# Second part in column halves: every leaf and outer product as two matmuls with 64 columns of weights

## The chip, the cores and the metric

The kernel runs on one core of a Trainium2 chip. What counts is the device time of one launch in microseconds (us), the median of several runs.

## The reference

Random-feature attention over 8 batches, 8 heads, 576 tokens and 64 features a head, then a Fourier mix and a feed-forward block on 8 x 576 = 4608 rows of 512 features, all in float32:

```python
q_p, k_p = phi(q_s), phi(k_s)                      # exp features, 128 of them
num = q_p @ (k_p^T v);  den = q_p @ sum(k_p) + 1e-06
x = num / den                                      # heads side by side: (8, 576, 512)
mixed = real(fft(fft(x, axis=1), axis=2))
u = x + mixed
un = (u - mean(u)) / sqrt(var(u) + 1e-06)
out = u + maximum(un @ w_ch1, 0) @ w_ch2           # 512 -> 2048 -> 512
```

Only the last line's two matrix products matter here.

## The kernel before

The program is written out by a planner of its own (`Listing`): steps with an engine and a planned time, in an order that is fixed by strings of picks. It is then issued in exactly that order, engine by engine, so a change inside a step does not move any other instruction. A matmul in float32 goes to the array as two weight loads and two matmuls, so the profile counts each call of `nc.tensor.matmul` twice; only transposes and bf16 matmuls count once.

The first part (to about 418 us) holds the attention, the Fourier mix, and the feed-forward of the first 4 tiles of 128 rows with plain products (L1236, L1259). The second part holds the feed-forward of the other 4096 rows, in 8 blocks of 512 (`j` = 0 to 7), with a fast matrix product of seven partial products in place of eight, on two levels: seven outer products (`i`), and within each seven inner ones (`n`), called leaves. Sums of weights and tokens are made beforehand by VectorE and GpSimd; the leaves add into PSUM banks, which ScalarE and VectorE copy, seed and combine.

- First layer, `first_of`: a leaf's matmuls contract over 128 input features. Blocks 0 and 1 are done alone: a leaf (L1727) is 4 matmuls with 128 columns of weights and 128 moving columns (tokens). Blocks 2 to 7 are done in pairs (`wide`): a leaf then has 256 moving columns and 2 matmuls, and is done twice (`g`) for the two halves of the hidden features. In block 0 six of the seven outer products have no inner level (`single`): L1878, 16 matmuls each with 256 moving columns.
- Second layer, `product_of`: a leaf (L2178) is 4 matmuls that add into the same 128 columns of a bank; its weights are 128 tokens' hidden values, its moving operand 128 columns of a `wl` tile that SyncE's queue loads (L2074) as buffers come free.

The steps between leaves: ScalarE saves a bank to SBUF (L1752, L2149), seeds another (L1759, L2194), VectorE adds a bank and a saved one (L2154, L1653, L1770), and a later leaf adds into the same bank. The last sums of hidden values (L1683) are on VectorE and GpSimd, tokens' sums on VectorE (L1358, L1456).

Ahead of the first leaves, `washed` (L2298) fills three banks by two bf16 matmuls each, on the whole array: four of the six stand before the first leaf, two after the second leaf.

Column halves and quarters of the array are in use in the first part: L735 and L701 work on quarters (64 rows by 64 columns of weights), L782 and L790 on column halves (128 rows by 64 columns, 65 moving), and L944 for the last group of frequencies on column halves with 128 and 129 moving columns. Two matmuls whose outputs lie in different halves of the partitions lie on different halves of the array's columns.

Of the kernel before, what the change touches and what calls it, by code (L numbers as in the profile page):

```python
# [375 lines left out]
def kernel(  # L376
# [10 lines left out]
    nc = tc.nc  # L387

    B, H, S, D = q.shape
# [13 lines left out]
    P = 128  # L403
# [663 lines left out]
    Q = 32  # L1067
# [45 lines left out]
    def normed(j, pool):  # L1113
# [12 lines left out]
        for i in range(TB // 128):  # L1126
            n, was = i + TB // 128 * (j - head(j)), head(head(j) - 1)
            yield Fork(paced(i), LEAF * (98 * was + 49 * len(unit(was)) * n // 8 - 8))

# [160 lines left out]

    tts = {}
    wxs, so = {}, {}
    LEAF = 0.9
    STORED = (1, 2, 5, 6, 3, 7, 4)
    PARTS = (1, 5, 2, 6, 3, 7, 4)
# [10 lines left out]
    def head(j):  # L1306

        return j - (j - WIDE) % 2 if wide(j) else j
# [380 lines left out]
    def first_of(j, i, g):  # L1689
        me = ("first", j, i, g)  # L1690
        cell_of = partial(here_of(j), g=g)
        span = 2 * P if wide(j) else P
# [16 lines left out]
        def leaf(n, ps, start, after=(), take=(), give=(), makes=None):  # L1709
            own = n in (5, 6, 3) and i != 1  # L1710
            w = ("wx", 1) if i == 1 else ("wx", j, i, n) if own else ("so", i, n)
            if wide(j) and (j, i) != (WIDE, 1):
                m = PARTS.index(n) + 7 * g
                own, w = m % 2, ("wx", j, i, m // 2)
            token = (("tokens", j, i),) if i != 1 else (("tt1" if wide(j) else "tt", j),)
            yield Step(
                PE, 0.866 if wide(j) else 0.895, after=token + (w,) + after, take=take, give=(("wl",) if own else ()) + give,
                makes=makes, bias=LEAF * PARTS.index(n),
            )
            b = None  # L1720
            if take:
                b, ps = got()
            elif isinstance(ps, str):
                ps = kept["y"][1]
            left, right = weights_of(j, i, n, g), tokens(j, i, n)
            for f in range(4 * P // span):
                nc.tensor.matmul(  # L1727
                    ps[:, span * f : span * f + span].rearrange("f (b q) -> f b q", q=Q),
                    lhsT=left[:, P * f : P * f + P],
                    rhs=right,  # L1730
                    start=start and f == 0,
                    stop=True,
                    skip_group_check=True,
                )
            return b, ps

        def made(f, t):
# [74 lines left out]
        if i in single(j):  # L1812
            def cells(n, f, c):
                return hid[:, n, f, :, 256 * c : 256 * c + 256]

            def halves_of(ps):
                return ps.rearrange("p (t n) -> p t n", t=2)


            unseeded = (0,) if not j and i == ORDER0[1] else ()  # L1820

            def out(f, c, b, ps):
                row = tuple(e for t in range(2) for e in over(f, t))
                here = (me, "half", f, c)
                if 2 * f + c in unseeded:
                    yield Step(DVE, 0.7, 0.1, after=free + row + with_(f, 0) + with_(f, 1), give=(b,), makes=here, bias=1.75)
                    relu_sum(cells(slot, f, c), halves_of(ps), cells(addend, f, c))
                    return
                yield Step(ACT, 0.6, 0.1, after=free + row, give=(b,) if i != 5 else (), makes=here, bias=1.75 * (2 * f + c + 1))
                nc.scalar.activation(out=cells(slot, f, c), in_=halves_of(ps), func=AF.Relu if final else AF.Copy)  # L1830

            def u4_of(f, c, b, ps):
                read = ((("second", j - 1, READ["u4"]), "read"),) if j else tuple(
                    ("h", j, n, f, t, g) for n in (2, 6) for t in range(2)
                )
                yield Step(
                    DVE, 0.7, 0.1, after=read + tuple(("h", j, 6, f, t, g) for t in range(2)) + ((me, "half", f, c),),
                    give=(b,), makes=("h", j, "u4 half", f, c), bias=1.75 * (2 * f + c + 1),
                )
                nc.vector.tensor_tensor(out=cells(C12, f, c), in0=halves_of(ps), in1=cells(C21, f, c), op=ALU.add)  # L1840

            def whole(f):
                here = tuple((me, "half", f, c) for c in range(2))
                if i != 5:
                    for t in range(2):
                        yield Step(NONE, after=here, makes=made(f, t))
                else:
                    here = tuple(("h", j, "u4 half", f, c) for c in range(2))
                    for t in range(2):
                        yield Step(NONE, after=here, makes=("h", j, "u4", f, t, g))  # L1850

            def seed_of(k):
                f, c = divmod(k, 2)
                after = with_(f, 0) + with_(f, 1) + (((me, "done", k - 2),) if k > 1 else ())
                yield Step(ACT, 0.6, 0.1, take=("clean",), after=after, makes=(me, "seed", k), bias=1.75 * k - 2)
                kept[k] = got()
                nc.scalar.activation(out=halves_of(kept[k][1]), in_=cells(addend, f, c), func=AF.Copy)

            for k in range(4 * merged):
                if k not in unseeded:  # L1860
                    yield Fork(seed_of(k))
            w, right = outer_weights(i), outer_tokens(j, i)
            for f in range(2):
                for c in range(2):
                    k = 2 * f + c
                    fresh = not merged or k in unseeded
                    seeded = () if fresh else ((me, "seed", k),)
                    yield Step(
                        PE, 1.73, after=(("tt", j),) + tuple(("sum", i, d, f) for d in range(2)) + seeded,
                        take=bank if fresh else (), give=("set",) if f and c else (),  # L1870
                        makes=(me, "done", k), bias=1.75 * k,
                    )
                    b, ps = got() if fresh else kept[k]
                    for n in range(2):
                        cell = ps.rearrange("p (t n) -> p t n", t=2)[:, :, 128 * n : 128 * n + 128]
                        for d in range(2):
                            col = GW * f + 256 * c + 128 * n
                            nc.tensor.matmul(  # L1878
                                cell.rearrange("f t (b q) -> f t b q", q=Q),
                                lhsT=w[:, d, col : col + 128],  # L1880
                                rhs=right[:, :, d].rearrange("f (t b) q -> f t b q", t=2),
                                start=fresh and n == 0 and d == 0,
                                stop=d == 1,
                                skip_group_check=True,
                            )
                    yield Fork(out(f, c, b, ps))
                    if i == 5:
                        yield Fork(u4_of(f, c, b, ps))
                yield Fork(whole(f))
            for n in ("leaves", "y"):  # L1890
                yield Step(NONE, after=((me, "done", 3),), makes=(me, n))
            return
# [80 lines left out]
    def w1_inner():  # L1973
# [19 lines left out]
        def replaced(i, a21):  # L1993
# [3 lines left out]
                makes=("so", i, 7),  # L1997
                bias=LEAF * (30 + 7 * m),
            )
# [31 lines left out]
    wls = {}  # L2031
# [80 lines left out]
    def product_of(j, i, cells):  # L2112
# [48 lines left out]
        def leaf(n, ps, left, start, after=(), give=(), take=(), makes=None):  # L2161

            shared = ((("second", j - 1, i), {5: "p5 read", 4: "read"}.get(n, n)),) if j != head(j) else ()
            yield Step(
                PE,
                0.895,
                after=(("wl", head(j), i, n),) + shared + after,
                take=take,
                give=(() if wide(j) and j == head(j) else tag_of(j, i, n)[:1]) + give,
                makes=makes or (me, n), bias=pace * LEAF * PARTS.index(n),  # L2170
            )
            b = None
            if take:
                b, ps = got()
            elif isinstance(ps, str):
                ps = saved["y"][1]
            for f in range(4):
                nc.tensor.matmul(  # L2178
                    ps[:, 0:128],
                    lhsT=left[:, f],  # L2180
                    rhs=wls[head(j), i, n][:, f],
                    start=start and f == 0,
                    stop=(f == 3),
                    skip_group_check=True,
                )
            return b, ps

        def of_sum(n):
# [206 lines left out]
```

## Time and profile before

| what | us |
|---|---|
| median of 3 runs | 1123.8 |
| lowest and highest | 1123.35, 1124.15 |
| span of the profiled execution | 1119.2 |
| TensorE matmuls busy | 1108.4 |
| TensorE weight loads busy | 1000.4 |
| VectorE busy | 888.7 |
| ScalarE busy | 539.5 |
| GpSimd busy | 390.6 |

The span runs from the first to the last instruction of the profiled execution; no other time is listed for that execution, and the median lies 4.6 us above its span. PE stands for TensorE's matmuls, PEld for its weight loads, DVE for VectorE, ACT for ScalarE, POOL for GpSimd, SPq for SyncE's DMA queue. A row of the timeline gives the start, the time from the first start to the last end, and how many instructions are merged; matmuls overlap, so the distance between starts is smaller than the duration of one. A form such as 128*64 128x129 means 128 rows and 64 columns of the array and a moving operand of 128 partitions and 129 columns.

### The profile page before, as it was taken

The page shows a single profiled execution, that of the slowest core. Times are in us where ns is not written, and L with a number is a line of the kernel's source. Part 1 is how long each engine was busy: PE and PEld are TensorE (multiplying, and loading weights), DVE is VectorE, ACT ScalarE, POOL GpSimd, SP SyncE. Part 2 cuts the span into 40 slices and gives each one's busy share as a digit, 9 for nine tenths or more (in the row PEclk, how much of TensorE's full clock was granted, in tenths as well). Part 3 has the DMA queues.
Part 4 walks back from the last instruction along what each step waited for, and adds up shares of the span by engine and source line. Part 5 has one row for each costly group of instructions (what it writes and reads, how often), then busy time and mean ns, then how long its engine had stood idle before and what let it go on. Part 6 is the DMA issues. An engine that isn't in the chain of part 4 may idle for free.

```text
span 1119.2 us, 31666 instructions
## 1 busy us (share of the span) xinstructions
PE 1108.4 (99%) x12467; PEld 1000.4 (89%) x12467; DVE 888.7 (79%) x1685; ACT 539.5 (48%) x1644; POOL 390.6 (35%) x401
## 2 busy tenths in 40 slices
PE   9999999999999999999999999999999999999998
PEld 7888888879868778999999889999889999889998
DVE  6999999987576767687697777888677888568895
ACT  7998898856536455623214452223463223331221
POOL 2443443553563348634413464000365000152000
PEclk9999999999999999999999999999999999999999
DMA  8856766665674669798896778747678656546453
GB/s 243 243 174 188 242 180 191 183 208 176 216 232 156 194 172 343 224 314 262 260 326 224 226 216 248 207 148 238 206 207 261 207 155 216 170 152 220 146 160 105
DMA packets 196549, 236.13 MB, mean 211 GB/s; under 512 B 53808, under 2 KB 120624, under 8 KB 196400
## 3 DMA queue, kind: packets, MB, share of 16 engines
q1 hardware_dynamic: 195904, 233.83, 68.1%
q8 instruction: 99, 1.62, 0.6%
q14 instruction: 50, 0.41, 0.1%
q10 hardware_dynamic: 496, 0.26, 0.1%
HBM read 182.13 MB, written 56.10 MB: 213 GB/s over the span
## 4 chain that ended last, share of the span: by engine, by line
PE 92%; DVE 3%; ACT 2%; DMA 2%; issue 0%; POOL 0%; SPq 0%; DVEq 0%; ACTq 0%
PE banks L2178 31%; PE banks L1727 27%; PE banks L1236 5%; PE banks L701 5%; PE banks L607 5%; PE banks L1259 5%; PE banks L1878 4%; PE banks L735 3%; PE banks L782 2%; PE banks L944 2%; PE banks L894 1%; ACT e L661 1%; DVE nmx L644 1%; PE banks L904 1%; DMA unw<-turned 1%; DMA raw<-in_moe_w_ch_dram 1%
## 5 line engine op out<-in xcount | busy, mean ns | idle before, releaser
L2178 PE MATMUL banks<-wl,sums 128*128 128x128 f32 x1792 | 219.8, 275 | 0.0
L2178 PEld LDWEIGHTS banks<-wl,sums 128*128 128x128 f32 x1792 | 210.6, 192 | 1.0 <-issue 0.3
L661 ACT ACTIVATE e<-banks,nmx 128x128 f32<-128x128 f32 x576 | 165.7, 441 | 23.3 <-DVE nmx L644 22.9
L644 DVE TENSOR_REDUCE nmx<-banks 128x8 f32<-128x1024 f32 (+1 forms) x96 | 89.3, 951 | 16.8 <-PE banks L701 12.4
L2178 PE MATMUL banks<-wl,hid 128*128 128x128 f32 x768 | 99.2, 275 | 0.3 <-DVE part L2154 0.3
L2178 PEld LDWEIGHTS banks<-wl,hid 128*128 128x128 f32 x768 | 92.8, 192 | 1.2 <-DVE part L2154 0.8
L2149 ACT ACTIVATE s<-banks 128x128 f32<-128x128 f32 x112 | 30.9, 277 | 113.6 <-PE banks L2178 103.5
L1727 PE MATMUL banks<-unw,wxw 128*128 128x256 f32 x352 | 85.4, 379 | 0.0
L701 PE MATMUL banks<-om,kqT 64*64 64x128 f32 (+1 forms) x2088 | 79.0, 275 | 1.7 <-ACT kv L751 1.3
L701 PEld LDWEIGHTS banks<-om,kqT 64*64 64x64 f32 (+1 forms) x2088 | 64.5, 138 | 12.7 <-issue 3.2
L2178 PE MATMUL banks<-wl,hx 128*128 128x128 f32 x576 | 74.2, 275 | 0.4 <-DVE part L2154 0.4
L1727 PEld LDWEIGHTS banks<-unw,wxw 128*128 128x128 f32 x352 | 66.6, 190 | 8.9
L1727 PE MATMUL banks<-rx,wxw 128*128 128x256 f32 x288 | 70.8, 379 | 0.0
L2178 PEld LDWEIGHTS banks<-wl,hx 128*128 128x128 f32 x576 | 69.4, 192 | 0.8 <-DVE part L2154 0.6
L1752 ACT ACTIVATE s<-banks 128x512 f32<-128x512 f32 x65 | 38.5, 596 | 65.1 <-PE banks L1727 60.0
L1727 PE MATMUL banks<-ttw,wxw 128*128 128x256 f32 x288 | 69.8, 379 | 0.0
L1236 PE MATMUL banks<-unT,w 128*128 128x128 f32 x512 | 65.4, 279 | 1.7 <-DVE qeT L621 1.7
L550 POOL TENSOR_TENSOR w<-w,raw 128x512 f32<-128x512 f32 x28 | 37.6, 1351 | 77.3 <-DVE raw L544 68.1
L2227 POOL TENSOR_TENSOR more<-more,part 128x512 f32<-128x512 f32 x2 | 2.6, 1315 | 176.6 <-ACT part L2220 176.6
L1236 PEld LDWEIGHTS banks<-unT,w 128*128 128x128 f32 x512 | 60.2, 192 | 4.5 <-issue 2.3
L1727 PEld LDWEIGHTS banks<-rx,wxw 128*128 128x128 f32 x288 | 54.5, 190 | 7.3
L1727 PEld LDWEIGHTS banks<-ttw,wxw 128*128 128x128 f32 x288 | 54.5, 190 | 7.3
(287 smaller groups left out, 2442.3 us busy)
## 6 DMA issues: line engine op xcount, KB each, us to landing
wl<-w2l SPq DMA_DIRECT2D x245, 256.0 KB, 3.9
wxw<-w1x SPq DMA_DIRECT2D x120, 256.0 KB, 3.1
raw<-in_moe_w_ch_dram SPq DMA_DIRECT2D x32, 512.0 KB, 4.8
kq<-in_k_dram SPq DMA_DIRECT2D x32, 288.0 KB, 4.5
kq<-in_q_dram SPq DMA_DIRECT2D x32, 288.0 KB, 4.5
vd<-in_v_dram SPq DMA_DIRECT2D x32, 288.0 KB, 5.4
ur<-us SPq DMA_DIRECT2D x30, 256.0 KB, 5.2
w2l<-sums SPq DMA_DIRECT2D x14, 512.0 KB, 4.9
```

The lines of the kernel that those rows point to most:

```text
L550: eng.tensor_tensor(out=dst, in0=dst, in1=lof, op=ALU.add)
L607: nc.tensor.transpose(ps[:, (j - j0) * 128 : (j - j0 + 1) * 128], src(j), ident[:])
L644: nc.vector.tensor_reduce(nmx[:, :, 0:num], pps[:, :, 0 : MF * num].rearrange("p b (c m) -> p b c m", m=MF), axis=AX.X, op=ALU.max, negate ...
L661: nc.scalar.activation(out=e[:, c + (i if num == 1 else 0), :], in_=pps[:, i, MF * c : MF * c + MF], func=AF.Exp, bias=nmx[:, i, c : c + 1],)
L701: nc.tensor.matmul(pps[cols, c, MF * m : MF * m + MF], lhsT=kqT[rows, j, cols], rhs=om2[rows, :],)
L735: nc.tensor.matmul(kvp[cols, i, 0 : D + 1], lhsT=feature(r)[rows, cols], rhs=vds[n % NV][rows, r, :], start=(r == 0), stop=(r == R - 1),)
L1236: nc.tensor.matmul(hp[:, 0:TP], lhsT=w1[:, dc, 128 * fc : 128 * fc + 128], rhs=unTs[key][:, dc, :], start=(dc == 0), stop=(dc == NDC - 1),)
L1259: nc.tensor.matmul(yp[:, 0:DM], lhsT=hs[fc][:, 128 * i : 128 * i + 128], rhs=w2[:, fc, :], start=(fc == 0), stop=(fc == NFC - 1),)
L1727: nc.tensor.matmul(ps[:, span * f : span * f + span].rearrange("f (b q) -> f b q", q=Q), lhsT=left[:, P * f : P * f + P], rhs=right, start ...
L1752: nc.scalar.activation(out=s[:], in_=ps, func=AF.Copy)
L1878: nc.tensor.matmul(cell.rearrange("f t (b q) -> f t b q", q=Q), lhsT=w[:, d, col : col + 128], rhs=right[:, :, d].rearrange("f (t b) q -> ...
L2178: nc.tensor.matmul(ps[:, 0:128], lhsT=left[:, f], rhs=wls[head(j), i, n][:, f], start=start and f == 0, stop=(f == 3), skip_group_check=True,)
```

## The change

Each of the three calls that make the second part's products becomes two, with 64 of the 128 weight columns each. The first writes partitions 0 to 63 of the output, the second 64 to 127. The moving operand is the same for both. The order of steps, the waits, the loads and all work of the other engines stay; `washed` stays on the whole array.

```diff
+    HALVES = (slice(0, D), slice(D, P))
...
             for f in range(4 * P // span):
-                nc.tensor.matmul(
-                    ps[:, span * f : span * f + span].rearrange("f (b q) -> f b q", q=Q),
-                    lhsT=left[:, P * f : P * f + P],
-                    rhs=right,
-                    start=start and f == 0,
-                    stop=True,
-                    skip_group_check=True,
-                )
+                for half in HALVES:
+                    nc.tensor.matmul(
+                        ps[half, span * f : span * f + span].rearrange("f (b q) -> f b q", q=Q),
+                        lhsT=left[:, P * f : P * f + P][:, half],
+                        rhs=right,
+                        start=start and f == 0,
+                        stop=True,
+                        skip_group_check=True,
+                    )
...
                             col = GW * f + 256 * c + 128 * n
-                            nc.tensor.matmul(
-                                cell.rearrange("f t (b q) -> f t b q", q=Q),
-                                lhsT=w[:, d, col : col + 128],
+                            for half in HALVES:
+                                nc.tensor.matmul(
+                                    cell[half].rearrange("f t (b q) -> f t b q", q=Q),
+                                    lhsT=w[:, d, col : col + 128][:, half],
...
             for f in range(4):
-                nc.tensor.matmul(
-                    ps[:, 0:128],
-                    lhsT=left[:, f],
+                for half in HALVES:
+                    nc.tensor.matmul(
+                        ps[half, 0:128],
+                        lhsT=left[:, f][:, half],
                         rhs=wls[head(j), i, n][:, f],
...
```

More of the change, by code (lines that the diff above doesn't have):

```diff
@@ L1877, in first_of @@
                             col = GW * f + 256 * c + 128 * n
-                            nc.tensor.matmul(
-                                cell.rearrange("f t (b q) -> f t b q", q=Q),
-                                lhsT=w[:, d, col : col + 128],
[L1881 to L1885, printed above, removed]
+                            for half in HALVES:
+                                nc.tensor.matmul(
+                                    cell[half].rearrange("f t (b q) -> f t b q", q=Q),
+                                    lhsT=w[:, d, col : col + 128][:, half],
+                                    rhs=right[:, :, d].rearrange("f (t b) q -> f t b q", t=2),
+                                    start=fresh and n == 0 and d == 0,
+                                    stop=d == 1,
+                                    skip_group_check=True,
+                                )
                     yield Fork(out(f, c, b, ps))
@@ L2177, in leaf @@
             for f in range(4):
-                nc.tensor.matmul(
-                    ps[:, 0:128],
-                    lhsT=left[:, f],
[L2181 to L2185, printed above, removed]
+                for half in HALVES:
+                    nc.tensor.matmul(
+                        ps[half, 0:128],
+                        lhsT=left[:, f][:, half],
+                        rhs=wls[head(j), i, n][:, f],
+                        start=start and f == 0,
+                        stop=(f == 3),
+                        skip_group_check=True,
+                    )
             return b, ps
```

## The prediction

> **What bounds the kernel now.** I read the page first (parts 1, 2 and 4), then the windows over the second part, then the chain of waits in order of time, then the timeline of TensorE at places where column halves are already in use.
>
> ```profile
> span 1119.2 us, 31666 instructions
> ...
> PE 1108.4 (99%) x12467; PEld 1000.4 (89%) x12467; DVE 888.7 (79%) x1685; ACT 539.5 (48%) x1644; POOL 390.6 (35%) x401
> ...
> PE 92%; DVE 3%; ACT 2%; DMA 2%; issue 0%; POOL 0%; SPq 0%; DVEq 0%; ACTq 0%
> ```
>
> TensorE is busy for 99% of the span and is 92% of the chain that ended last. The change touches only the second part, which begins at about 417.8 us. First all engines in three windows, then the longest of them for lines L1727 and L2178 alone (columns: stretch, its length, busy us and count of each engine, granted clock, DMA share, GB/s), then TensorE's waits in it.
>
> ```profile
> 417.80:1119.20 701.40, 697.06 (x4956) 660.20 (x4954) 542.26 (x922) 239.16 (x593) 204.64 (x194) 1.00 0.71 218
> 418.00:550.00 132.00, 132.00 (x1001) 126.40 (x1001) 96.84 (x146) 56.52 (x125) 72.74 (x57) 1.00 0.87 279
> 550.00:600.00 50.00, 49.70 (x424) 48.68 (x424) 43.33 (x72) 9.18 (x37) 13.84 (x10) 1.00 0.99 307
> ...
> 417.80:1119.20 701.40, 309.93 (x1624) 273.36 (x1624) 1.00 0.71 218
> ...
> 417.80:1119.20 701.40, 357.04 (x3136) 355.12 (x3136) 1.00 0.71 218
> ...
> PE banks L2178 <- DVE part L2154: 0.7, 2, 0.4
> ```
>
> The reader is to see that in 701.4 us TensorE waited 0.7 us, at a full clock (1.00). So the time of this part is the number of matmul passes times the distance between their starts. Every matmul of the code appears as two loads and two matmuls: L2178 has 8 blocks x 49 leaves x 4 = 1568 of them in the code and 3136 in the row. I call each of the two a pass. By the code 1176 of the 1624 passes of L1727 have 256 moving columns (3 pairs of blocks x 49 leaves x 2 x 2, times two passes) and 448 have 128; the 192 of L1878 (6 products x 16 x two passes) have 256. That makes 3136 + 448 = 3584 passes of 128 columns and 1368 of 256. The distances stand in long unbroken pieces of the chain (start, us, what, count):
>
> ```profile
> 310.49 1.97 PE banks L607 x18
> ...
> 403.81 13.73 PE banks L1259 x32
> ...
> 686.62 81.29 PE banks L2178 x728
> ...
> 774.91 78.57 PE banks L1727 x364
> ```
>
> A pass of 128 columns takes 81.29 / 728 = 0.11166 us, one of 256 takes 78.57 / 364 = 0.21585, one of 512 (L1259) 13.73 / 32 = 0.42906. Between 256 and 512 a column costs 0.21321 / 256 = 0.000833 us; that line gives 0.10925 at 128. The pass of 128 is 2.4 ns above it. The transposes (L607), also 128 columns on the whole array, take 1.97 / 18 = 0.1094 and lie on the line. What differs between L607 and L2178 is the load:
>
> ```profile
> L2178 PEld LDWEIGHTS banks<-wl,sums 128*128 128x128 f32 x1792 | 210.6, 192 | 1.0 <-issue 0.3
> ...
> L607 PEld LDWEIGHTS banks<-ident,kq 128*128 128x128 f32 x288 | 32.2, 141 | 7.5 <-issue 2.7 <-ACT e L661 1.8 <-DMA kq<-in_q_dram 0.4
> L701 PEld LDWEIGHTS banks<-om,kqT 64*64 64x64 f32 x1872 | 50.9, 133 | 10.1 <-issue 2.2 <-ACT kv L751 1.7 <-ACT kqT L623 1.4
> ```
>
> 192 ns against 141, and a load of 64 columns takes 133. So I read a 128-column pass with ordinary weights as paced by its load of 128 columns, not by its moving columns; a 256-column pass is paced by its moving columns.
>
> **The change part by part.** It removes the 128-column loads: each pass becomes two, with 64 columns of weights, on the two column halves of the array. TensorE issues 9904 more instructions (4952 loads, 4952 matmuls). Order, waits, steps, banks, DMAs and the work of the other engines stay as they are. The question is what a pair of half passes costs. The trace has two near forms, shown in the timeline (start, us from the first start to the last end, what, count): the quarters of L701 (64 x 64 weights, 128 moving columns; of each four, two and two share their moving operand) and L944 on column halves.
>
> ```profile
> 168.81 1.32 PE L701 MATMUL banks<-om,kqT 64*64 64x128 f32 x40
> 170.07 0.66 PE L607 MATMUL banks<-ident,e 128*128 128x128 f32 x4
> ...
> 170.67 1.95 PE L1236 MATMUL banks<-unT,w 128*128 128x128 f32 x16
> 172.55 1.98 PE L701 MATMUL banks<-om,kqT 64*64 64x128 f32 x64
> 174.35 1.23 PE L735 MATMUL banks<-vd,e 64*64 64x65 f32 x72
> ...
> 74.51 0.27 PE L944 MATMUL banks<-cd_sb,y 128*64 128x129 f32 x1
> 74.52 0.27 PE L944 MATMUL banks<-sd_sb,y 128*64 128x129 f32 x1
> 74.62 0.28 PE L944 MATMUL banks<-cd_sb,y 128*64 128x128 f32 x1
> 74.63 0.28 PE L944 MATMUL banks<-sd_sb,y 128*64 128x128 f32 x1
> ```
>
> In L944 the two halves start 0.01 apart and the next pair 0.11 after the first: the halves run beside each other, 128 rows deep, which is the form of the change. In L701 40 matmuls are 10 rounds of four and 64 are 16; 1.98 - 1.32 = 0.66 for 6 rounds is 0.110 a round (0.108 to 0.112 with the rounding).
>
> For 128 moving columns I take 0.1093 for a pair: the line gives 0.10925, L607 0.1094, L701 0.110. Saved: 0.11166 - 0.1093 = 0.0024, times 3584 = 8.6 us. The bounds are 0.112 (L701's upper rounding, nothing saved, 1.2 us lost) and 0.108 (13 us saved); with 0.110 itself it is 5.9. I lean on the line because its rows are 32 to 728 passes long and L701's difference is 6 rounds.
>
> For 256 columns no row shows a half pass. Its time stands on the line by which I judge, so it has no load to shed: saved 0. From both sides: the offset of the second half, up to 0.01 in the rows of L944, if it weren't hidden; below, nothing, since the moving columns remain.
>
> **What is added.** The array changes between whole and halves. All of the second part is then in halves but the six bf16 matmuls of L2298, which stand before the first leaf and between the second and third: three changes, where there was none. L1236 at 170.67 has its last start at 170.67 + 1.95 - 0.275 = 172.345; L701 starts at 172.55, 0.205 later, 0.095 more than a round, and its 16 rounds hold 1.98 - 15 x 0.110 - 0.29 (the last one and the stagger of four) = 0.04 more. The other way, L701's last start 169.86 to 170.07 is 0.21, again 0.10 over, and L607's four hold 0.66 - 3 x 0.1094 - 0.272 = 0.06 over. Three changes: 0.14 + 0.16 + 0.14 = 0.4 us.
>
> Issue costs nothing: L701 passes four matmuls and four loads per 0.110, and here it is two and two. Their fetching is small too:
>
> ```profile
> q8 instruction: 99, 1.62, 0.6%
> ...
> SPq L2074 <- PE banks L2178: 133.7, 121, 5.9
> ```
>
> 1.62 MB for about 25,000 instructions grows by 0.6 MB to 0.8% of the DMA engines, as dense per us as in the first part. The weight loads of the second layer (L2074) wait for TensorE to free a buffer 121 times, so they move forward with it. VectorE is busy 542.26 of 701.4 us, 77%, and would be 78%.
>
> **The sum.** -8.6 + 0.4 = -8.2 us. The profiled execution has a span of 1119.2; the median is 1123.8, that is 4.6 around it, which the change doesn't touch. 1123.8 - 8.2 = 1115.6 us (span 1111.0).
>
> **A rule against it.** The rows of L607 and L2178 differ by 2.3 ns a pass, with the load as the visible difference. The Trainium skill (TensorE: Matmul & The Clock Gate, LDWEIGHTS) gives a load as its columns over 1.2 GHz, 107 ns for 128, which as an estimate is under the 109 of the moving columns: by that the load is hidden already and the sum would be +0.4, 1124.2. The trace doesn't bear it out, by those 2.3 ns; the case is the first rival.
>
> **The rivals.**
>
> First, the load is hidden already, and the 2.4 ns are something that stays, such as adding into PSUM, which L607 doesn't do. Then only the changes of the array remain: 1124.2, no change. Against it: L735 adds in quarters over nine rounds, and its 72 matmuls (18 rounds of 65 columns) take 1.23; less 0.29 for the last one and the stagger of four that is 0.94 / 17 = 0.055 a round, under the 0.057 that 65 columns cost on the line. Adding shows no price there. 0.07.
>
> Second, the slower side: a pair costs its offset. The second half starts up to 0.01 behind the first; in L701 and L944 that is hidden, but each of their matmuls has cells of its own, while the four of a leaf add into the same ones. If the offset showed at 0.007, a 128 pair would be 0.1163, 4.6 ns more than now, and a 256 pair 7 ns more: 16.5 + 9.6 + 0.4 = 26.5, 1150.3. It decides from 8.2 / 4952 = 1.7 ns per pair. L735's rounds speak against it too, though at half the columns. 0.08.
>
> Third, a half's load can't run under a matmul of the other half, and each pass shows a 64-column load: at half of 0.11166, 0.056 x 4952 = 277 us, about 1400. L944's pairs at 0.11 speak against it. 0.02. The Trainium skill (TensorE: Matmul & The Clock Gate, What overlaps and what doesn't) says that a load overlaps matmuls in flight only when the row groups differ, and two column halves have the same rows; this trace disagrees, by 0.11 a pair.
>
> Fourth, TensorE gets faster and something else holds. The place is 550 to 600 us, with the DMA share at 0.99 and VectorE at 43.33 of 50. If that stretch kept its end, the 128-column passes before it (1001 less about 200 of 256) and in it (some 400) would give back 1200 x 0.0024 = 2.9 us: 1118.5. 0.08.
>
> **How the numbers follow.** About 0.2% (2.2 us) is what a measurement of this kernel tells from no change. The forecast, 1113.5 to 1118.5 (L701's 0.110 gives 1118.3), has 0.75; with the fourth rival, up to 1121, faster is 0.83; the first is 0.07, no change; the second and third are 0.10, slower. 1113.5 to 1121 leaves the first three rivals out, 0.17, and a little below: the lower end is the pair at 0.1087, between L701's 0.108 and the line. So 1115.6, 1113.5 to 1121.
>
> **What would show it.** In the chain of the changed kernel, a long piece of L2178 of n matmuls should last n / 2 x 0.1093, and one of L1727 with 256 columns n / 2 x 0.216. The loads of L2178 should be near 138 ns, not 192. TensorE should show 17,419 matmuls, and its waits should still be about 1 us. I am wrong if a 128 pair takes 0.1117 or more (first or second rival), if a 256 pair takes over 0.218, or if waits of several us stand before L2178 or L1727.

## The result, and the profile after

| | median us | lowest and highest | ratio to the kernel before, 95% interval |
|---|---|---|---|
| before (6 runs) | 1123.68 | 1121.91, 1124.15 | |
| changed (6 runs) | 1117.41 | 1114.02, 1119.45 | 0.9943 [0.9926, 0.9960] |

The changed kernel is faster by 6.3 us in these medians; 8.2 was forecast. Two later sets of runs give 6.2 and 6.7 us (e1_again and e12_after_third, below). Lines move by one to four: L1727 is now L1729, L1878 L1881, L2178 L2182, L2298 L2302, L2154 L2157, L1683 L1684, L1770 L1772.

The page of the changed kernel:

```profile
span 1112.2 us, 41566 instructions
...
PE 1099.9 (99%) x17419; PEld 939.9 (85%) x17419; DVE 889.4 (80%) x1685; ACT 539.9 (49%) x1644; POOL 391.5 (35%) x401
...
q8 instruction: 137, 2.24, 0.9%
...
PE 91%; DVE 4%; ACT 3%; DMA 1%; issue 1%; DVEq 0%; SPq 0%
...
L2182 PEld LDWEIGHTS banks<-wl,sums 128*64 128x64 f32 x3584 | 202.1, 137 | 2.1 <-issue 0.5
```

TensorE has the 17,419 matmuls, is still busy for 99% of the span, and a load takes 137 ns where it took 192. The chain of waits of the changed kernel, at the same two long pieces (start, us, what, count):

```profile
685.38 79.53 PE banks L2182 x1456
...
771.84 78.56 PE banks L1729 x728
```

The first holds 728 pairs, 79.53 / 728 = 0.10924 us each (before 0.11166). The second holds 364 pairs of 256 columns, 0.21582 each (before 0.21585). By the starts of single matmuls over the whole second part, which resolve more than the rows, it is 0.10918 against 0.11165, and 0.21584 against 0.21588. TensorE's waits in the second part of the changed kernel (total, times, longest):

```profile
PE banks L2182 <- DVE part L2157: 0.9, 2, 0.5
PE banks L1881 <- DVE so L1684: 0.8, 1, 0.8
```

The first row was there before; the second is new. The ends of the second part stand in the timeline of TensorE, of before and then of the changed kernel:

```profile
417.38 0.60 PE L2298 MATMUL banks<-ident 128*128 128x256 bf16 x4
...
421.61 1.06 PE L1727 MATMUL banks<-unT,w1s 128*128 128x128 f32 x8
...
1114.39 1.16 PE L2178 MATMUL banks<-wl,hx 128*128 128x128 f32 x8 [0.39 <-DVE part L2154]
```

```profile
417.65 0.60 PE L2302 MATMUL banks<-ident 128*128 128x256 bf16 x4
...
422.20 1.04 PE L1729 MATMUL banks<-unT,w1s 128*64 128x128 f32 x16
...
1107.51 1.09 PE L2182 MATMUL banks<-wl,hx 128*64 128x128 f32 x16 [0.39 <-DVE part L2157]
```

From the first L2298 to the start of the last matmul it is 1114.39 + 1.16 - 0.275 - 417.38 = 697.9 us before and 1107.51 + 1.09 - 0.273 - 417.65 = 690.7 after. Below, "the second part" is always this length. It is 7.2 us shorter. 3584 passes saved 3584 x 0.00247 = 8.85; the three changes of the array lie between the first two rows of each fence, four leaves of 8 passes among them: 4.55 - 4.23 + 32 x 0.00247 = 0.40 us for the three; the waits grew by 1.0. That makes -7.45; 0.2 us are not assigned.

**Where the new wait comes from.** The matmuls of L1881 at 428 us need the weight sums `so`, which VectorE and GpSimd make. VectorE and GpSimd in the timeline, before and then changed:

```profile
425.93 2.35 DVE L1683 TENSOR_TENSOR so<-so,w 128x512 f32<-128x512 f32 x2
...
425.95 1.78 POOL L1683 TENSOR_TENSOR so<-w,so 128x512 f32<-128x512 f32 x1
```

```profile
425.89 0.69 DVE L1772 TENSOR_TENSOR hid<-banks,s 128x512 f32<-128x512 f32 x1 [1.63 <-PE banks L1729]
426.50 4.90 DVE L1684 TENSOR_TENSOR so<-so,w 128x512 f32<-128x512 f32 x3
...
426.24 1.27 POOL L1684 TENSOR_TENSOR so<-w,so 128x512 f32<-128x512 f32 x1
```

In the kernel before, VectorE's sum starts within 0.02 us of GpSimd's. Its two sums then take 2.35 us and GpSimd's takes 1.78. In the changed kernel VectorE comes 0.26 later than GpSimd, since its `hid` waits for a leaf (L1729) that the changes of the array have delayed; GpSimd's then takes 1.27, and VectorE's first two sums 3.16 (the chain of waits has them as `DVE so L1684 x2`). So in both profiles the sums slow each other, and the one that starts first is the less hindered. The 0.8 us of the two sums is the 0.8 us of the wait. Other profiles show the same at this place: in e4, e5 and the twin of before (e10) VectorE starts within 0.02 us of GpSimd and TensorE doesn't wait; in e1, e8 and e12 it starts 0.27 to 0.30 later and TensorE waits. In e2 VectorE starts 0.65 later and no such wait is listed: TensorE itself comes to these matmuls 0.7 us later there than in the changed kernel, by its added changes of the array. An order of these sums in which VectorE goes first was not tried.

### The profile page after: what moved, and what is told of

Its sections match the earlier page's. It is cut to its first block, busy times and chain, and to the rows that moved or that the text cites. A ratio compares the mean times of both kernels' runs of the same rounds, so it can differ in the third digit from the quotient of the medians.

```text
span 1112.2 us, 41566 instructions
## 1 busy us (share of the span) xinstructions
PE 1099.9 (99%) x17419; PEld 939.9 (85%) x17419; DVE 889.4 (80%) x1685; ACT 539.9 (49%) x1644; POOL 391.5 (35%) x401
## 4 chain that ended last, share of the span: by engine, by line
PE 91%; DVE 4%; ACT 3%; DMA 1%; issue 1%; DVEq 0%; SPq 0%
PE banks L2182 30%; PE banks L1729 27%; PE banks L1236 5%; PE banks L701 5%; PE banks L607 5%; PE banks L1259 5%; PE banks L1881 4%; PE banks L735 2%; PE banks L782 2%; PE banks L944 2%; ACT e L661 2%; PE banks L894 1%; DVE nmx L644 1%; PE banks L904 1%; PE banks L955 1%
## 5 line engine op out<-in xcount | busy, mean ns | idle before, releaser
L2182 PE MATMUL banks<-wl,sums 128*64 128x128 f32 x3584 | 217.9, 273 | 0.1
L2182 PEld LDWEIGHTS banks<-wl,sums 128*64 128x64 f32 x3584 | 202.1, 137 | 2.1 <-issue 0.5
L2182 PE MATMUL banks<-wl,hid 128*64 128x128 f32 x1536 | 99.3, 273 | 0.5 <-DVE part L2157 0.5
L2182 PEld LDWEIGHTS banks<-wl,hid 128*64 128x64 f32 x1536 | 88.1, 137 | 2.2 <-DVE part L2157 1.1
L1729 PE MATMUL banks<-unw,wxw 128*64 128x256 f32 x704 | 86.5, 379 | 0.0
L701 PE MATMUL banks<-om,kqT 64*64 64x128 f32 (+1 forms) x2088 | 79.3, 276 | 1.4 <-ACT kv L751 0.7
L701 PEld LDWEIGHTS banks<-om,kqT 64*64 64x64 f32 (+1 forms) x2088 | 64.8, 139 | 12.6 <-issue 3.6
L2182 PE MATMUL banks<-wl,hx 128*64 128x128 f32 x1152 | 73.8, 273 | 0.4 <-DVE part L2157 0.4
L1729 PEld LDWEIGHTS banks<-unw,wxw 128*64 128x64 f32 x704 | 54.0, 137 | 21.3
L1729 PE MATMUL banks<-rx,wxw 128*64 128x256 f32 x576 | 71.7, 379 | 0.0
L1729 PE MATMUL banks<-ttw,wxw 128*64 128x256 f32 x576 | 70.6, 379 | 0.0
L2182 PEld LDWEIGHTS banks<-wl,hx 128*64 128x64 f32 x1152 | 65.8, 137 | 1.2 <-DVE part L2157 0.6
L1729 PEld LDWEIGHTS banks<-rx,wxw 128*64 128x64 f32 x576 | 44.0, 137 | 17.7
L1729 PEld LDWEIGHTS banks<-ttw,wxw 128*64 128x64 f32 x576 | 43.9, 137 | 17.7
```

Of the source, the lines that this page charges most:

```text
L701: nc.tensor.matmul(pps[cols, c, MF * m : MF * m + MF], lhsT=kqT[rows, j, cols], rhs=om2[rows, :],)
L1729: nc.tensor.matmul(ps[half, span * f : span * f + span].rearrange("f (b q) -> f b q", q=Q), lhsT=left[:, P * f : P * f + P][:, half], rhs= ...
L2182: nc.tensor.matmul(ps[half, 0:128], lhsT=left[:, f][:, half], rhs=wls[head(j), i, n][:, f], start=start and f == 0, stop=(f == 3), skip_gr ...
```

## The experiments

**Which of the forms pays: halves only at 128 columns, halves only at 256.**

```diff
 # e2_only128
-                for half in HALVES:                                    # first_of
+                for half in HALVES if span == P else (slice(0, P),):
-                            for half in HALVES:                        # outer products, 256 columns
+                            for half in (slice(0, P),):
 # e3_only256
-                for half in HALVES:                                    # first_of
+                for half in HALVES if span != P else (slice(0, P),):
-                for half in HALVES:                                    # product_of, 128 columns
+                for half in (slice(0, P),):
```

> Halves only where 128 columns move; the passes with 256 columns stay whole. Theory (the 128-column load paced the 128-column pass, a pass of 256 columns had nothing to gain): pairs at 0.1092, passes of 256 at 0.2158 as in both kernels, but now 57 changes between whole and halves instead of three. At 0.14 us each, as estimated in the prediction, 54 more cost 7.6 us and eat nearly the whole 8.8: about 1123 (second part about 698 us). Rival (changing the array is cheaper than that, since loads run ahead): under 0.05 us each, 1115 to 1118.

> Halves only where 256 columns move; the passes with 128 columns stay whole at 0.1117. Theory: nothing is saved, and 54 changes of the array at 0.14 us cost 7.6 us: about 1131. Rival (the 256-column halves bring part of the gain): under 1127.

e2 took 1123.85 us, ratio 1.0013 [1.0003, 1.0023]; e3 1131.53, ratio 1.0080 [1.0066, 1.0093]. In e2 a 128 pair takes 0.10917 by its starts and a whole pass of 256 columns 0.2158; in e3 a whole pass of 128 takes 0.11167 and a 256 pair 0.21583. So the halves save at 128 columns alone, and what else these kernels add is their 57 and 54 changes between whole and halves. One of them can be read from a stretch where the two forms alternate; the chain of waits of e2, then of before at the same leaves:

```profile
774.73 1.93 PE banks L1729 x8
776.66 1.02 PE banks L2182 x16
777.68 1.92 PE banks L1729 x8
```

```profile
769.67 1.73 PE banks L1727 x8
771.40 0.89 PE banks L2178 x8
```

In e2 a first-layer leaf and a second-layer leaf together take 777.68 - 774.73 = 2.95 us. Without changes they would take 1.73 + 8 x 0.1092 = 2.60: two changes cost 0.35, one 0.17. Over the whole second part e3 is 707.1 - 697.9 = 9.2 us longer for 54 changes, 0.17 each. The split by direction, from the starts in e2, is 0.14 into halves and 0.20 back. That is why the change is worth making only if nearly everything in the part is in halves: e2 keeps all of the saving and gives it back in changes.

**Load or adding: what paced a pass of 128.** e4 is the kernel before, whole array, with 96 of the 128 weight columns in L2178, so that 32 of each leaf's 128 output rows are left out. e5 is the kernel before, each of a leaf's four matmuls overwriting.

```diff
 # e4_cols96
-                    ps[:, 0:128],
-                    lhsT=left[:, f],
+                    ps[0:96, 0:128],
+                    lhsT=left[:, f][:, 0:96],
 # e5_noadd
-                    start=start and f == 0,
-                    stop=(f == 3),
+                    start=True,
+                    stop=True,
```

> The kernel before, with 96 instead of 128 columns of weights in each matmul of the second layer's leaves, on the whole array, no halves; 32 of the 128 output rows of each leaf are left out. Theory (the load of 128 weight columns paces the pass): a load of 96 is short enough, the pass falls to 0.1092, the second layer's 3136 passes save 7.6 us: about 1116. Rivals (adding into the same cells, or the two tiles side by side, make the difference): 0.1117 per pass, 1123.7 as before.

> The kernel before, whole array, 128 columns of weights; each of the four matmuls of a second-layer leaf overwrites the cells instead of adding to them (the sums over hidden features and the additions onto earlier leaves are left out). Theory (the load paces the pass): nothing changes, 0.1117 per pass, about 1122.5. Rival (adding into the same cells costs the 2.4 ns): the pass falls to 0.1093, 7.5 us less, about 1115.

The chain of waits of e4 and a row of its page, then the chain of e5, the same piece of 728 passes:

```profile
685.90 79.47 PE banks L2178 x728
...
L2178 PEld LDWEIGHTS banks<-wl,sums 128*96 128x96 f32 x1792 | 202.7, 163 | 1.4 <-issue 0.4
```

```profile
689.88 81.29 PE banks L2178 x728
```

e4: 79.47 / 728 = 0.1092 a pass, on the whole array, with adding, without a pair. It took 1114.81 us, ratio 0.9937 [0.9922, 0.9950]. e5: 81.29 / 728 = 0.11166, as before; 1122.50, ratio 0.9993 [0.9981, 1.0005]. So neither the halves nor the adding made the 2.5 ns, but the load of 128 columns: with 96 columns or with 64 it no longer shows in the 0.1092 that 128 moving columns take. Since e4 also writes fewer output rows, a fixed cost of writing 128 rows would explain it too; but then a whole pass of 256 columns, which writes 128 rows as well, would be slower than a pair of halves, and it is not (0.21588 against 0.21584). The Trainium skill (TensorE: Matmul & The Clock Gate, LDWEIGHTS) has a load last its columns over 1.2 GHz, 107 ns for 128, which would be hidden; here a stream of such loads paces at 111.65 ns, and the measurement decides.

**Must the two halves be neighbours in the queue?** e6 is the changed kernel with the four matmuls of the first half ahead of the four of the second, in the second layer.

```diff
-            for f in range(4):
-                for half in HALVES:
+            for half in HALVES:
+                for f in range(4):
```

> The changed kernel, but a second-layer leaf issues its four matmuls of the first column half and then its four of the second, in place of first, second, first, second. Theory (matmuls start in the order in which they are issued, so two halves run side by side only when they are neighbours in the queue): eight passes of one half run alone, then eight of the other, with an overlap of one at each seam, so a leaf takes about 14 pair times in place of 8, 1.53 us for 0.875; 392 leaves give 257 us more, about 1374. Rival (each half has a queue of its own and runs ahead): 0.875 us a leaf, about 1116 as the changed kernel.

1162.08 us, ratio 1.0351 [1.0324, 1.0378]: neither of the two expectations. The chain of e6 and a few rows of its timeline of TensorE:

```profile
698.84 89.59 PE banks L2182 x1449
```

```profile
720.17 0.27 PE L2182 MATMUL banks<-wl,sums 128*64 128x128 f32 x1
720.22 0.27 PE L2182 MATMUL banks<-wl,hx 128*64 128x128 f32 x1
720.28 0.27 PE L2182 MATMUL banks<-wl,sums 128*64 128x128 f32 x1
720.33 0.27 PE L2182 MATMUL banks<-wl,hx 128*64 128x128 f32 x1
```

The piece is the 91 leaves that were 79.53 us in the changed kernel: 0.985 us a leaf, 9 pair times rather than 8 (the 1449 are 1456 with seven records missing). Matmuls of two leaves (`sums` and `hx`) alternate 0.055 apart, though all of one leaf stand ahead of the other's in the queue: one half begins a leaf while the other half still ends the one before. So passes that stand four apart in the queue (two matmuls of the code) still run beside each other, and a leaf is as long as if one of its passes found no partner: 0.11 us x 392 leaves = 43 us, of the 1162.1 - 1117.4 = 44.7 measured.

**Does issue cost nothing? Four column quarters.** e9 is the changed kernel with each product as four matmuls of 32 weight columns.

```diff
-                for half in HALVES:
+                for half in [slice(32 * k, 32 * k + 32) for k in range(4)]:     # in all three products
```

> All three products as four matmuls with 32 columns of weights on the four column quarters. Theory (at 64 columns the load is off the path and the moving columns pace the pass): no further gain, four quarter passes in 0.1092 for 128 columns and 0.2158 for 256, since four matmuls and four loads per 0.110 are what the quarters of the first part do; second part 690.7 us as with halves, time about 1116. Rival (a load still costs a part of the pass): under 0.1085, 3 us or more gained; or issue binds at 128 rows: 0.112 or more, 1124.

A miss: 1191.70 us, ratio 1.0620 [1.0599, 1.0641]. Its page, waits and chain:

```profile
PE 1125.3 (95%) x27323; PEld 962.6 (81%) x27323; DVE 890.0 (75%) x1685; ACT 539.5 (45%) x1644; POOL 390.5 (33%) x401
...
q8 instruction: 215, 3.52, 1.3%
```

```profile
PE banks L2182 <- issue: 39.9, 53, 2.6
PE banks L1729 <- issue: 8.7, 10, 2.3
```

```profile
732.24 3.69 PE banks L2182 x127
735.93 0.33 issue
736.26 3.70 PE banks L2182 x127
739.96 0.85 issue
740.80 3.73 PE banks L2182 x128
...
757.93 0.60 issue
758.53 1.49 PE banks L2182 x41
```

By the starts a round of four still takes 0.109 us where TensorE has work, but these two rows list 63 waits, 48.6 us in all. They count a wait from the modelled end of the last matmul; from start to start there are 86 steps over 0.3 us, and they lengthen the second part by 74 us, nearly all of the 75.6 by which it is longer than with halves. In the chain a stop stands after every 127 or 128 matmuls, that is 256 instructions with their loads, and an instruction packet of q8 is 3.52 MB / 215 = 16.4 kB. From 732.24 to 758.53 six such blocks (764 matmuls, 1528 instructions) take 26.29 us, 17 ns an instruction. Quarters need one every 13.7 ns (8 in 0.109), halves one every 27. So it fits that TensorE's instructions arrive at 17 ns each in such a stretch, and that halves can be fed at this and quarters can't. A stretch of e9 where most quarters have 256 moving columns bears it out: from 632 to 731 us TensorE takes about 2100 matmuls with as many loads, 24 ns an instruction, and has no wait. That it is their fetching is argued from the step of 256. The Trainium skill (Runtime: NRT & Kernel Launch, Instruction fetch mechanics) has the fetch in blocks of 256 instructions, which agrees, and hidden because issue is slower, which these stops, if they are the fetching, do not bear out.

**The three remaining changes of the array.** e7 is the changed kernel with L2298 in halves too, so that the second part has no change of array inside; e11 is the same kernel again.

```diff
         for h in range(2):
+            for half in HALVES:
-                ps[:, 256 * h : 256 * h + 256], lhsT=eye[:, 0:128], ...
+                ps[half, 256 * h : 256 * h + 256], lhsT=eye[:, half], ...
```

> The changed kernel with the six bf16 matmuls of L2298 in column halves too, so that two of the three changes of the array at the start of the second part disappear (the one after the plain products remains). Theory: about 0.3 us earlier up to 428 us, but there the changed kernel now waits 0.9 us for a weight sum on VectorE (L1684), which doesn't move; the wait grows by the same amount and the second part from the plain products' end to the last matmul stays as long, within 0.1 us. Rival (the wait moves with TensorE): 0.3 us shorter. Time 1115 to 1118 in both.

> The version with the bf16 matmuls in halves once more, for its time: it showed 1114.6 (four runs, 1113.3 to 1115.9) where the changed kernel had 1116.3 to 1117.4. From its profile the second part from the last plain product's start is 0.2 to 0.5 us shorter. If that is all, the median lies between 1115.5 and 1117; if two changes of the array cost more than the profile shows, 1113.5 to 1115.

e7: 1114.60 us, ratio 0.9923 [0.9901, 0.9944]; e11: 1116.16, ratio 0.9946 [0.9927, 0.9966]. Together they can't be told from the changed kernel. The second part of e7 is 690.3 us, 0.3 shorter. The wait for `so` neither grew, as I had expected of a faster start, nor went; a second one of 0.2 us, put down to a DMA, now stands just ahead of it. VectorE and GpSimd in the timeline of e7:

```profile
428.21 5.14 DVE L1684 TENSOR_TENSOR so<-so,w 128x512 f32<-128x512 f32 x3
...
428.19 1.27 POOL L1684 TENSOR_TENSOR so<-w,so 128x512 f32<-128x512 f32 x1
```

Here VectorE is again within 0.02 us of GpSimd, as in the kernel before, yet it is GpSimd that isn't hindered (1.27). At such a tie the traces differ by nanoseconds: GpSimd starts 6 to 15 ns ahead in e4, e5 and e10 and is hindered all the same, 23 and 26 ns ahead in e11 and e7 and is not. What decides is not shown.

**The changed kernel again.**

> The changed kernel once more, as it is. Its six runs lie between 1114.0 and 1119.5, those of the kernel before between 1121.9 and 1124.2, so what is open is where 5 us of spread come from. If the pace of the passes varies (a pair of 128 columns above 0.1093 us in some executions), the profile of a slower execution shows long pieces of the second layer over 0.1093 per pair. If waits vary, the pieces keep 0.1092 and TensorE's waits grow from 1.7 us to 4 or 6. Median expected 1115 to 1118, second part 690.7 us from the first bf16 matmul to the last matmul's start.

> The changed kernel beside the three others on the same chip, so that the versions share the runs of the kernel before. 1115 to 1118; second part 690.7 to 691; if a weight load lands late around 570 us in the profiled execution, a wait of 1 us or more on it and a granted clock under 1.00 in the window 566 to 580.

e1: 1116.29 us (1115.34 to 1120.70), ratio 0.9955 [0.9938, 0.9973], second part 690.9, 128 pairs at 0.10918, the same waits and one of 0.2 us for a weight tile. e12: 1116.02 (1114.38 to 1118.51), ratio 0.9936 [0.9923, 0.9949]. The profiled execution of e12 is the longest of its runs, 4.5 us over that of the first profile, and shows where: its first L2302 starts at 420.82 us, not 417.65, ahead of anything that was changed, and its second part is 692.0, with 0.8 us of small waits at 573 and 580 us.

**What makes some executions longer.** In two profiles of this family, of executions at the top of their runs (e2 with 1126.00, e11 with 1121.95), TensorE waits near 572 us for a weight tile of the second layer. The waits of e2 and of e11, then the window 566 to 580 us in e11 and in the changed kernel:

```profile
PE banks L2182 <- DMA wl<-w2l: 1.8, 1, 1.8
```

```profile
PE banks L2182 <- DMA wl<-w2l: 2.5, 1, 2.5
```

```profile
566.00:580.00 14.00, 11.05 (x169) 10.60 (x166) 9.07 (x13) 1.87 (x9) 3.15 (x2) 0.88 0.90 280
```

```profile
566.00:580.00 14.00, 13.54 (x246) 13.13 (x243) 12.77 (x24) 2.25 (x10) 1.09 (x1) 1.00 1.05 299
```

In e11 169 matmuls fit where the changed kernel has 246, and the granted clock is 0.88. After the wait of 2.5 us the pairs take 0.213 us, twice their time, for about 3.3 us. Together that makes the second part of e11 694.7, 4 us longer. To see whether these loads spread the times, e8 (the changed kernel) and e10 (the kernel before) load only half of each weight tile of block 1's second layer and use that half twice; the other half of those products is left out.

```diff
-                    nc.sync.dma_start(wl[:].rearrange("p f m -> p (f m)"), w2l[i][STORED.index(l)])
+                    part = slice(0, 256 if j == 1 else 512)
+                    nc.sync.dma_start(wl[:].rearrange("p f m -> p (f m)")[:, part], w2l[i][STORED.index(l)][:, part])
-                        rhs=wls[head(j), i, n][:, f],
+                        rhs=wls[head(j), i, n][:, f % 2 if j == 1 else f],
```

> The changed kernel, but in block 1's second layer only half of each weight tile is loaded (49 loads of 128 KB for 256 KB) and used twice; the other half of its products is left out. TensorE's passes are the same. It takes load off the DMA engines around 545 to 590 us, where their share is at 1. Theory on the spread of the changed kernel's times (1114 to 1121): in the slower executions a load of the second layer lands late there, TensorE waits 1 to 2 us and then runs some 3 us at half clock, as the kernel of the 128-column halves alone showed it. Then the times of this kernel lie within 2 us of each other, near 1114.5, with no wait on a weight load. Rival (the spread comes from the first part or from the whole run): still 4 to 5 us between lowest and highest.

> The kernel before with half of each weight tile of block 1's second layer loaded and used twice; the other half of those products is left out. Twin of the light version of the changed kernel, whose six times lay within 2 us (1115.1 to 1117.1) where the full one had 5. If late loads around 570 us make the spread of the kernel before as well, its times lie within 2 us, near 1121.5, in place of 1120.2 to 1126.3; the difference of the two light kernels is then 7 us, that of the second parts in the profiles (697.9 less 690.5). If the spread is of the first part: 1120 to 1126 as before, and a difference of 6.

e8: 1116.01 us (1115.12 to 1117.07, six runs), ratio 0.9936 [0.9919, 0.9953], second part 690.5, no wait for a weight tile. e10: 1123.59 (1120.93 to 1125.83, twelve runs), ratio 1.0005 [0.9993, 1.0016], second part 697.9. Between these two the medians differ by 7.6 us and the second parts by 7.4. For the changed kernel this fits that late weight tiles lengthen some executions (a spread of 2 us, against 4 to 5.4 in three sets of it), but six runs don't show it. For the kernel before it does not: the spread of e10 is as wide as that of before, and no profile of it shows such a wait.

## Why the prediction was right, point by point

- *A pass of 128 columns falls from 0.11166 to 0.1093, 8.6 us.* Right: 0.10918 by the starts, 8.85 us. e4, e5 and the unchanged 256-column passes show the reason as it was given, the load.
- *A pass of 256 columns keeps its time.* Right: 0.21584 against 0.21588, and in e3 0.21583. The second half's offset doesn't show.
- *Three changes of the array, 0.14 + 0.16 + 0.14.* Right as a sum, 0.40 measured. Between two products of the second part, in e2 and e3, a change costs 0.17; the term taken from L701 and L607 was a little low for them.
- *Issue and fetching cost nothing.* Right for halves (the share of q8 rose to 0.9%, 0.8% was forecast), but its ground was too weak. The 4 + 4 instructions per 0.110 of L701 are a burst of 16 rounds, 128 instructions. Kept up, that rate doesn't hold, as e9 shows; the margin of the halves is 27 ns against 17 per instruction, not what the burst suggested.
- *TensorE's waits stay at about 1 us.* This term was mis-sized: 1.7 us against 0.7. I looked at VectorE's share of time (77%) and at the stretch with the most DMA, not at the sums on which TensorE's next matmul depends right behind the changes of array. At 428 us the kernel before has almost no slack: its two sums end at 425.93 + 2.35 = 428.28, and in its chain of waits the matmuls that follow begin at 428.34. With the delay of the array changes GpSimd became the earlier one there.
- *The sum.* 8.2 us was forecast; the second part shows 7.2 in the profiles, and the medians 6.2 to 6.7. The missing 1.0 of the first difference is the growth of the waits, the new one for the most part. That the medians show less than the profiles is not clear of noise: the interval of the first ratio is 4.5 to 8.3 us. What lengthens single executions has three shown places. One is the first part, which ends between 417.4 and 421.2 us in the profiles, and nearly as late in a kernel without halves (420.6 in e5). One is a late weight tile near 570 us. The third lies outside the span, in the next point. How much of the median each makes is open.
- *4.6 us around the span.* Not so: for the profiled execution of the changed kernel both times are known, 1114.02 and 1112.2, so 1.8 lie around the span. In the 51 runs of the kernel before that are listed with their spans it is 1.7 to 1.8 in every one, so its profiled execution took about 1121.0 and was a short one too. Nor is it a constant that the change doesn't touch: in the 18 listed runs of the changed kernel it is 1.8 to 3.3. Why is open. The forecast from the median didn't depend on it, the span that was named did only in its difference: 1111.0 forecast, 1112.2 measured.

The rivals. The first (the load is hidden already, something else stays) fell with e4, where the load was made smaller on the whole array and the whole gain came, and with e5. The second (a pair pays its offset) fell with the 256 pairs. The third (a half's load can't run under the other half) fell with 0.1092 a pair; e6 shows that the two halves need not even be neighbours. The fourth (550 to 600 us keeps its end) did not occur in the first profile, which has the pairs at full rate there, but its place was well chosen: the late weight tiles of e2 and e11 lie in it, and cost 4 us in e11.

## What to carry to other kernels

Where an engine is never idle, divide long unbroken pieces of its chain by their counts, compare forms that differ in one property, and a difference of 2 ns per instruction becomes a sum that can be trusted; a variant such as e4, which takes away the suspected property and little else, tells the cause. Count what every switch between forms costs (here 0.17 us) before a form is used in part of a stage: the same saving was worth 6 us with three switches and nothing with 57. A steady rate of instructions has to be taken from a long piece, not from a burst, and two engines that start within 0.02 us of each other are a place to check when everything ahead of them moves by a few tenths.

## What the runs showed of the hardware that I had not expected

- Column halves are independent to a depth of at least four passes: in e6 a half runs on to the next leaf while the other is still at this one, and only about the time of one pass per leaf is lost (0.985 us a leaf for 0.874).
- Quarters with 13.7 ns per instruction starve TensorE in steps of 256 instructions, at 17 ns each (e9); halves, at 27 ns, don't.
- A wait of TensorE of 1.8 to 2.5 us was followed by about 3.3 us at half rate (e2, e11), so that the 2.5 us of e11 cost about 4. The waits of 0.8 and 0.5 us in the second part of the changed kernel were not followed by that.
- A VectorE sum of 128 x 512 that meets a GpSimd sum takes 1.5 to 1.8 us, alone 0.69, and GpSimd's 1.8 in place of 1.27. GpSimd goes unhindered where it starts 0.023 us or more ahead of VectorE, VectorE where GpSimd is at most 0.015 ahead, so the time of the pair turns on some 0.01 us.
